# Extraction of V's diagonal blocks in two Vector instructions, and w2 over four column groups in pieces of 4, 5 and 1 rows

## The chip, the cores and the metric

The kernel runs on one NeuronCore of a Trainium2 chip. The metric is the device time of one execution in microseconds (us); lower is better. The engines are named as the profile names them: PE (matrix products; PEld is its weight load), DVE (the Vector engine), ACT (the Scalar engine), POOL (GpSimd) and SP (the queue that issues nearly all DMAs).

## The reference, cut to what matters

The kernel computes one decode step of a gated mix of an attention block and a dense block, for a batch of two rows with 512 features, in bf16:

```
g   = sigmoid(sum(x * gate_w))                      # one gate per batch row
q   = x @ wq                                        # 32 heads of 128
p   = softmax(q . k_cache / sqrt(128))              # 4096 keys per head
a   = (p . v_cache) @ wo                            # wo is 4096 x 512
h   = relu(x @ w1)                                  # 1376 wide
b   = h @ w2                                        # w2 is 1376 x 512
out = g * a + (1 - g) * b                           # 2 x 512
```

The K cache and the V cache hold 64 MB each (2 x 32 heads x 4096 keys x 128 features). All inputs together are about 145 MB, and each byte is used once.

## The kernel before, in words

**Staging.** K and V come in 16 units of 4 MB each (four heads to a unit), K's first, into three slots of `kv`. `wq` comes ahead of them. SP issues every one of these transfers in the order of a list (lines 260 to 271): the transfer of unit n waits until unit n-3 has released its slot, which for a V unit is the marker `pe_v_{v}`, the end of its matrix products. After the last V unit SP issues, without any further wait of its own kind, the last 96 rows of `w2` (`w2a`, line 267), `wo` in two halves (`wo0`, `wo1`, lines 268 and 269), and then the first 1280 rows of `w2` in three pieces (`w2b`, `w2c`, `w2d`, lines 270 and 271). In the tile `w2` a "row" is one slice `w2[:, r, :]` of 128 partitions by 512 columns; `w2b` holds rows 0 to 3, `w2c` rows 4 to 7, `w2d` rows 8 and 9, and row 10 is `w2a`.

**Order.** The program is written out by hand as one list of operations for each engine; an operation waits for named markers of other engines (`waits`) and for the semaphores of transfers (`dwaits`). Each engine works through its list in order.

**K stage.** DVE transposes the 4 MB of a unit in four steps (line 379), PE computes scores from them (lines 385 and 406).

**V stage.** After the softmax, `v_unit(v)` issues 32 matrix products of 512 columns each (line 456) for each V unit. They go to four column groups of the array in turn (group t writes PSUM partitions 32t to 32t+15), so that four run side by side. The result is one PSUM bank of 128 x 512 in which only some 128-column blocks are wanted: for each partition one of four. `v_extract(v)` picks it out with four DVE instructions on 128 columns each: the first multiplies block 0 by column 0 of the mask `maskc` (line 467), each of the next three multiplies block c by column c and adds what is there already (line 470). The result goes to `X2`.

**Where V's transfers are waited for.** For units 1 to 12 the wait for a unit's transfer stands not at its first matrix product on PE but at the last extraction instruction of the unit before, on DVE (line 472); PE waits for that instruction. For units 0 and 13 to 15 the first matrix product itself waits for the transfer (line 459). `o_gather(0)` is issued after unit 8: PE gathers batch row 0's eight results (line 484), DVE scales them (line 488), PE moves them to 128 partitions (line 492), DVE copies them (line 495).

**The end.** After unit 15 come `o_gather(1)`, then `project()`: DVE clears a PSUM bank (line 499), PE multiplies by `wo` in 32 products of 512 columns over four column groups (line 503), rows 16 to 31 of them behind `wo1`, and DVE copies the bank to `pr_sb` (line 506). `ffn_f()` multiplies by `w2`: for each row `fin_row` issues two products of 256 columns, in column groups 0 and 1 (line 510). The order is row 10, rows 0 to 3, then a product of `sel2` with `pr_sb` in float32 that adds the attention's part, then rows 4 to 9. `store()` casts the two halves to bf16, one on DVE (line 524) and one on ACT (line 525), and SP writes 2 KB out (line 272).

Of the kernel before, what the change touches and what calls it, by code (L numbers as in the profile page):

```python
# [4 lines left out]
ALU = mybir.AluOpType  # L5
ACT = mybir.ActivationFunctionType
AX = mybir.AxisListType
# [78 lines left out]
def bass_gated_mix__gqa_block_cached__dense_activation_relu__decode_kernel(  # L86
# [48 lines left out]
    pr_sb = sb("pr_sb", [128, 512], dt.float32)  # L135
# [4 lines left out]
    maskc = sb("maskc", [128, 4], dt.float32)  # L140
# [3 lines left out]
    X2 = sb("X2", [128, 2, 8, 128], dt.float32)  # L144
# [3 lines left out]
    out_sb = sb("out_sb", [2, 512], dt.bfloat16)  # L148
# [6 lines left out]
    def psf(p0, p1, c0, n):  # L155
        return PSF[p0:p1, c0:c0 + n]

    BANK = 512
    V_B = 6
# [9 lines left out]
    FIN_C0 = 0  # L169
# [5 lines left out]
    sem = {n: nc.alloc_semaphore("sem_" + n) for n in names}  # L175
# [4 lines left out]
    def marker(name):  # L180
        m = mk.get(name)
        if m is None:
            m = _Marker()
            mk[name] = m
        return m
# [5 lines left out]
    def slot_of(what):  # L191
        return place[what] % NSLOT

    def slot_wait(what):
        return (sem_slot[slot_of(what)], 16 * (place[what] // NSLOT + 1))

    def freed(what):
        kind, u = what
        return marker(f"kt_{4 * u + 3}") if kind == "k" else marker(f"pe_v_{u}")
# [5 lines left out]
    def dve(fn, waits=(), signal=None, dwaits=()):  # L205
        P.add("dve", fn, waits=[marker(w) for w in waits], signal=marker(signal) if signal else None, dwaits=dwaits)

    def act(fn, waits=(), signal=None, dwaits=()):
        P.add("act", fn, waits=[marker(w) for w in waits], signal=marker(signal) if signal else None, dwaits=dwaits)

    def pe(fn, waits=(), signal=None, dwaits=()):
        P.add("pe", fn, waits=[marker(w) for w in waits], signal=marker(signal) if signal else None, dwaits=dwaits)
# [5 lines left out]
         waits=["c_i16z"], signal="c_i16")  # L218
# [5 lines left out]
                                   in_=mask3[:].rearrange("p (t f) h c -> p t f h c", t=4)[:, :, 0],  # L224
                                   pattern=[[-32, 4], [-4, 4], [-1, 4]],
                                   compare_op=ALU.not_equal, fill=1.0, base=0, channel_multiplier=1),
         waits=["c_m3z"], signal="c_m3")
# [3 lines left out]
         waits=["c_s1"], signal="c_s2")  # L231
    pool(lambda g: g.affine_select(out=sell[:], in_=sell[:], pattern=[[16, 2], [2, 8], [32, 4]],
                                   compare_op=ALU.is_ge, fill=0.0, base=1, channel_multiplier=-1),
         waits=["c_s2"], signal="c_sell")
# [3 lines left out]
         waits=["c_s4z"], signal="c_s4")  # L238
# [16 lines left out]
    def sp(fn, waits=(), dwaits=()):  # L255
        P.add("sp", fn, waits=waits, dwaits=dwaits)
# [4 lines left out]
    for n, what in enumerate(order):  # L261
        waits = [freed(order[n - NSLOT])] if n >= NSLOT else []
        sp(lambda e, what=what: e.dma_start(kv[:, slot_of(what), :], unit_in(what)).then_inc(sem_slot[slot_of(what)], 16),
           waits=waits)
# [2 lines left out]
    sp(lambda e: e.dma_start(w2[0:96, 10, :], B_w2[1280:1376, :]).then_inc(sem["w2a"], 16))  # L267
    sp(lambda e: e.dma_start(wreg[:, 0:8192], wo_in[:, 0:8192]).then_inc(sem["wo0"], 16), waits=[marker("pe_h")])  # L268
    sp(lambda e: e.dma_start(wreg[:, 8192:16384], wo_in[:, 8192:16384]).then_inc(sem["wo1"], 16))
    for name, r0, r1 in (("w2b", 0, 4), ("w2c", 4, 8), ("w2d", 8, 10)):  # L270
        sp(lambda e, name=name, r0=r0, r1=r1: e.dma_start(w2[:, r0:r1, :], w2a_in[:, r0:r1, :]).then_inc(sem[name], 16))
    sp(lambda e: e.dma_start(out.rearrange("b s n -> (b s) n"), out_sb[:, :]).then_inc(sem["out"], 16),
       waits=[marker("dve_out"), marker("act_out")])
# [171 lines left out]
    def v_unit(v):  # L445
        grp, u4 = divmod(v, 4)
        what = ("v", v)
        rows = kv[:, slot_of(what), :].rearrange("p (a c r d) -> p a c r d", a=2, c=4, r=16)
        for n in range(32):
            a, r16 = divmod(n, 16)  # L450
            t = n % 4
            waits = []
            if n == 0:
                waits = [f"pt{grp}_{hq}" for hq in range(4)] if u4 == 0 else []
                waits += [f"dve_x{v - 1}_3"] if v >= 1 else ["dve_v0"]
            pe(lambda e, n=n, t=t, a=a, r16=r16, grp=grp, u4=u4, rows=rows: e.matmul(  # L456
                psf(32 * t, 32 * t + 16, V_B * BANK, 512), lhsT=ptm[:, grp % 2, r16, u4, a, :, :],
                rhs=rows[:, a, :, r16, :], start=(n < 4), stop=(n >= 28), tile_position=(0, 32 * t)),
               waits=waits, dwaits=([slot_wait(what)] if n == 0 and not 1 <= v <= 12 else []), signal=(f"pe_v_{v}" if n == 31 else None))

    def v_extract(v):
        b, u8 = divmod(v, 8)
        for c in range(4):
            src = psf(0, 128, V_B * BANK + 128 * c, 128)
            dst = X2[:, b, u8, :]
            if c == 0:
                dve(lambda e, src=src, dst=dst: e.tensor_scalar(out=dst, in0=src, scalar1=maskc[:, 0:1], scalar2=None, op0=ALU.mult),  # L467
                    waits=[f"pe_v_{v}", "dve_maskc"], signal=f"dve_x{v}_0")
            else:
                dve(lambda e, src=src, dst=dst, c=c: e.scalar_tensor_tensor(out=dst, in0=src, scalar=maskc[:, c:c + 1], in1=dst,  # L470
                                                                            op0=ALU.mult, op1=ALU.add),
                    waits=[f"dve_x{v}_{c - 1}"], dwaits=([slot_wait(("v", v + 1))] if c == 3 and v <= 11 else []), signal=f"dve_x{v}_{c}")


    def o_denominators():
        pe(lambda e: e.matmul(psf(0, 64, L_C0, 1), lhsT=sell[:].rearrange("p b u h -> p (b u h)"), rhs=lrow[:, :], start=True, stop=True),
# [5 lines left out]
    def o_gather(b):  # L482
        for u in range(8):
            pe(lambda e, u=u, b=b: e.matmul(psf(0, 32, O_C0, 128), lhsT=selx[:, 28 - 4 * u:60 - 4 * u], rhs=X2[:, b, u, :],  # L484
                                            start=(u == 0), stop=(u == 7)),
               waits=[f"dve_x{8 * b + u}_3"] + (["dve_rinv", "dve_selx"] if u == 0 else []),
               signal=(f"pe_O{b}" if u == 7 else None))
        dve(lambda v, b=b: v.tensor_scalar(out=O_sb[:, b, :], in0=psf(0, 32, O_C0, 128), scalar1=rinv[:, b:b + 1],  # L488
                                           scalar2=gb[0:32, b:b + 1], op0=ALU.mult, op1=ALU.mult),
            waits=[f"pe_O{b}", "dve_rinv", "dve_g"], signal=f"dve_O{b}")  # L490
        for dq in range(4):
            pe(lambda e, dq=dq, b=b: e.matmul(psf(0, 128, R_C0 + 32 * b, 32), lhsT=s4[:, dq, :], rhs=O_sb[:, b, 32 * dq:32 * dq + 32],  # L492
                                              start=(dq == 0), stop=(dq == 3), tile_position=(0, 0)),
               waits=([f"dve_O{b}", "c_s4"] if dq == 0 else []), signal=(f"pe_R{b}" if dq == 3 else None))
        dve(lambda v, b=b: v.tensor_copy(out=oW[:, :, b], in_=psf(0, 128, R_C0 + 32 * b, 32)), waits=[f"pe_R{b}"], signal=f"dve_oW{b}")
# [10 lines left out]
        dve(lambda v: v.tensor_copy(out=pr_sb[:, :], in_=psf(0, 128, PR_C0, 512)), waits=["pe_pr"], signal="dve_pr")  # L506

    def fin_row(first, last, lhsT, rhs, dw, waits, signal):
        for c in range(2):
            pe(lambda e, c=c: e.matmul(psf(32 * c, 32 * c + 2, FIN_C0, 256), lhsT=lhsT, rhs=rhs[:, c * 256:(c + 1) * 256],  # L510
                                       start=first, stop=last, tile_position=(0, 32 * c), skip_group_check=True),
               dwaits=(dw if c == 0 else []), waits=(waits if c == 0 else []), signal=(signal if c == 1 else None))

    def ffn_f():
        for n, r in enumerate([10, *range(10)]):
            m = 96 if r == 10 else 128
            dw = {10: [(sem["w2a"], 16)], 0: [(sem["w2b"], 16)], 4: [(sem["w2c"], 16)], 8: [(sem["w2d"], 16)]}.get(r, [])
            if r == 4:
                fin_row(False, False, sel2[:, :], pr_sb, [], ["dve_pr", "dve_sel2"], None)
            fin_row(n == 0, r == 9, hT[0:m, r, :], w2[0:m, r, :], dw, ["dve_h0", "dve_h1"] if n == 0 else [],  # L520
                    "pe_fin" if r == 9 else None)

    def store():
        dve(lambda v: v.tensor_copy(out=out_sb[:, 0:256], in_=psf(0, 2, FIN_C0, 256)), waits=["pe_fin"], signal="dve_out")
        act(lambda a: a.activation(out=out_sb[:, 256:512], in_=psf(32, 34, FIN_C0, 256), func=ACT.Copy), waits=["pe_fin"],  # L525
            signal="act_out")


    gate()
# [7 lines left out]
    for v in range(16):  # L537
        if v == 2:
            o_denominators()
        if v % 4 == 0 and 4 <= v <= 8:  # L540
            sm_spread(v // 4 + 1)
        v_unit(v)
        if v == 1:
            ffn_h()
            ffn_relu()
        v_extract(v)
        if v == 8:
            o_gather(0)
    o_gather(1)
    project()  # L550
    ffn_f()
    store()

    P.resolve()
# [30 lines left out]
```

## Time and profile before

| what | value |
|---|---|
| median of 3 runs | 346.12 us (346.08, 346.12, 346.93) |
| the profiled execution: its own time | 346.78 us |
| its span (first to last instruction) | 345.4 us |
| PE, DVE busy share of the span | 58%, 53% |
| DMA: bytes read, mean rate | 145.43 MB, 421 GB/s |
| hardware queue q1, share of 16 DMA engines | 98.3% |
| granted PE clock, mean | 0.822 of full speed |

The profile's durations come from the one profiled execution. The 1.38 us between its time and its span lie outside what the trace shows. In the timeline a row is a run of like instructions: start, stretch in us, engine, line, operation, output and inputs, how many, and in brackets how long the engine idled before it and what ended the idle time.

### The profile page before, as it was taken

The page shows a single profiled execution, that of the slowest core. Times are in us where ns is not written, and L with a number is a line of the kernel's source. Part 1 is how long each engine was busy: PE and PEld are TensorE (multiplying, and loading weights), DVE is VectorE, ACT ScalarE, POOL GpSimd, SP SyncE. Part 2 cuts the span into 40 slices and gives each one's busy share as a digit, 9 for nine tenths or more (in the row PEclk, how much of TensorE's full clock was granted, in tenths as well). Part 3 has the DMA queues.
Part 4 walks back from the last instruction along what each step waited for, and adds up shares of the span by engine and source line. Part 5 has one row for each costly group of instructions (what it writes and reads, how often), then busy time and mean ns, then how long its engine had stood idle before and what let it go on. Part 6 is the DMA issues. An engine that isn't in the chain of part 4 may idle for free.

```text
span 345.4 us, 2397 instructions
## 1 busy us (share of the span) xinstructions
PE 201.0 (58%) x1203; PEld 40.2 (12%) x830; DVE 184.4 (53%) x167; ACT 15.0 (4%) x50; POOL 25.7 (7%) x32
## 2 busy tenths in 40 slices
PE   0429877878788687878780773233445343232365
PEld 0200000000000000000000241000113111000132
DVE  0848998999998999999978121111111201111121
ACT  1040000000000000000004000000000000000000
POOL 8400000000000000000002400400040000000000
PEclk9999998999999999999997565665557866655678
DMA  8999999999999999999999999999999999999994
GB/s 312 452 436 436 429 423 425 433 429 440 440 433 431 422 425 425 436 436 436 433 423 425 433 431 440 433 429 435 429 425 429 435 425 436 436 434 433 392 417 190
DMA packets 5748, 145.58 MB, mean 421 GB/s; under 512 B 645, under 2 KB 746, under 8 KB 1130
## 3 DMA queue, kind: packets, MB, share of 16 engines
q1 hardware_dynamic: 5732, 145.43, 98.3%
q8 instruction: 8, 0.13, 0.2%
q10 hardware_dynamic: 6, 0.00, 0.0%
q14 instruction: 2, 0.02, 0.0%
HBM read 145.43 MB, written 0.00 MB: 421 GB/s over the span
## 4 chain that ended last, share of the span: by engine, by line
DMA 73%; DVE 18%; PE 7%; issue 1%; SPq 1%; ACT 0%; DVEq 0%
DMA kv<-in_A_k_cache_dram 36%; DMA kv<-in_A_v_cache_dram 27%; DVE kt L379 15%; DMA wreg<-in_A_wo_dram 10%; PE PS L456 5%; DVE mpad L414 1%; PE PS L510 1%; DVE kt L427 1%; DVE ptm L440 1%; PE PS L503 1%; DVE X L470 0%; PE PS L385 0%; SPq L267 0%; PE PS L406 0%; SPq L268 0%
## 5 line engine op out<-in xcount | busy, mean ns | idle before, releaser
L379 DVE STREAM_TRANSPOSE kt<-kv 128x2048 f32<-128x2048 f32 x64 | 142.3, 2280 | 18.9 <-DMA kv<-in_A_k_cache_dram 18.9
L385 PE MATMUL PS<-kt,qbuf 128*128 128x512 bf16 x373 | 106.7, 393 | 0.3
L456 PE MATMUL PS<-kv,ptm 128*16 128x512 bf16 x512 | 55.9, 616 | 85.0 <-DVE X L470 57.1
L406 PE MATMUL PS<-kt,qbuf 128*128 128x512 bf16 x128 | 51.1, 399 | 33.5 <-DVE kt L379 32.9
L467 DVE TENSOR_SCALAR X<-PS,maskc 128x128 f32<-128x128 f32 x16 | 5.6, 350 | 67.8 <-PE PS L456 67.8
L470 DVE SCALAR_TENSOR_TENSOR X<-PS,maskc,X 128x128 f32<-128x128 f32 x48 | 16.8, 351 | 46.0 <-DMA kv<-in_A_v_cache_dram 44.7
L442 POOL COPY ptm<-kt 32x512 bf16<-32x512 bf16 x13 | 14.4, 1111 | 232.7 <-DVE lrow L428 175.5
L456 PEld LDWEIGHTS PS<-kv,ptm 128*16 128x16 bf16 x512 | 16.4, 124 | 123.9 <-issue 68.9
L406 PEld LDWEIGHTS PS<-kt,qbuf 128*128 128x128 bf16 x128 | 12.6, 98 | 147.5 <-DVE kt L379 106.6
L349 ACT ACTIVATE qbuf<-PS 32x4 bf16<-32x4 bf16 x32 | 5.7, 179 | 76.6 <-PE PS L385 76.0
L525 ACT ACTIVATE out_sb<-PS 2x256 bf16<-2x256 f32 x1 | 0.4, 375 | 154.6 <-PE PS L510 154.6
L424 ACT ACTIVATE kt<-PS,negm 128x512 bf16<-128x512 f32 x4 | 2.7, 685 | 80.7 <-DVE negm L421 80.7
L279 PE MATMUL PS<-ident,x_sb 3*128 3x3 bf16 x4 | 0.3, 166 | 8.1 <-DMA x_sb<-in_gate_w_dram 8.1
L282 DVE COPY xT<-PS 128x12 bf16<-128x12 bf16 x1 | 0.2, 170 | 8.4 <-PE PS L279 8.4
L503 PE MATMUL PS<-wreg,oW 128*2 128x512 bf16 x32 | 2.9, 500 | 2.9 <-DMA wreg<-in_A_wo_dram 2.0
L220 POOL MEMSET qbuf<- 128x5120 bf16 x1 | 4.4, 4370 | 0.0
L484 PE MATMUL PS<-X,selx 128*32 128x128 f32 x32 | 4.0, 273 | 0.1
L284 DVE COPY xTw<-xT 128x8 bf16<-128x8 bf16 x1 | 4.0, 3973 | 0.0
L365 DVE TENSOR_SCALAR hT<-PS,gm 128x10 bf16<-128x10 f32 x2 | 0.5, 226 | 6.3 <-PE PS L359 6.3
L492 PE MATMUL PS<-O_sb,s 32*128 32x32 bf16 x8 | 0.5, 182 | 5.5 <-DVE O_sb L488 5.5
L318 PE MATMUL PS<-wreg,xTw 128*32 128x512 bf16 x32 | 3.6, 628 | 0.0
L285 DVE TENSOR_TENSOR xg<-xT 128x8 f32<-128x8 bf16 x1 | 3.6, 3630 | 0.0
(66 smaller groups left out, 49.5 us busy)
## 6 DMA issues: line engine op xcount, KB each, us to landing
kv<-in_A_k_cache_dram SPq DMA_DIRECT2D x16, 4096.0 KB, 20.6
kv<-in_A_v_cache_dram SPq DMA_DIRECT2D x16, 4096.0 KB, 25.0
wreg<-in_A_wq_dram SPq DMA_DIRECT2D x1, 4096.0 KB, 12.4
wreg<-in_A_wo_dram SPq DMA_DIRECT2D x2, 2048.0 KB, 31.7
wreg<-in_B_w_dram SPq DMA_DIRECT2D x1, 1376.0 KB, 23.1
w<-in_B_w_dram SPq DMA_DIRECT2D x2, 512.0 KB, 35.1
w<-in_B_w_dram SPq DMA_DIRECT2D x1, 256.0 KB, 35.6
w<-in_B_w_dram SPq DMA_DIRECT2D x1, 96.0 KB, 25.4
```

Of the source, the lines that this page charges most:

```text
L220: pool(lambda g: g.memset(qbuf[:], 0.0), signal="c_qbuf")
L284: dve(lambda v: v.tensor_copy(out=xTw[:, :, 0:2], in_=xT), waits=["dve_xT", "c_xTw"], signal="dve_xTw")
L349: act(lambda a, out=out, src=src: a.activation(out=out, in_=src, func=ACT.Copy), waits=[f"pe_sc_{4 * uh + 3}"], signal=f"q_1_{uh}_{hq}")
L379: dve(lambda v: v.transpose(out=dst, in_=pairs[:, h, 64 * rr:64 * rr + 64, :]), waits=([f"pe_sc_{i - NKT}"] if i >= NKT else []), dwaits=( ...
L385: return e.add_instruction(mybir.InstMatmult(start_tensor_calc=start, stop_tensor_calc=stop, tile_size=(128, 128), tile_position=(0, 0), l ...
L406: return e.matmul(out, lhsT=lhsT, rhs=rhs, start=start, stop=stop)
L442: pool(lambda e, dst=dst, src=src: e.tensor_copy(out=dst, in_=src), waits=waits, signal=f"pt{g}_{hq}")
L456: pe(lambda e, n=n, t=t, a=a, r16=r16, grp=grp, u4=u4, rows=rows: e.matmul(psf(32 * t, 32 * t + 16, V_B * BANK, 512), lhsT=ptm[:, grp % 2, ...
L467: dve(lambda e, src=src, dst=dst: e.tensor_scalar(out=dst, in0=src, scalar1=maskc[:, 0:1], scalar2=None, op0=ALU.mult), waits=[f"pe_v_{v}" ...
L470: dve(lambda e, src=src, dst=dst, c=c: e.scalar_tensor_tensor(out=dst, in0=src, scalar=maskc[:, c:c + 1], in1=dst, op0=ALU.mult, op1=ALU.add),
L484: pe(lambda e, u=u, b=b: e.matmul(psf(0, 32, O_C0, 128), lhsT=selx[:, 28 - 4 * u:60 - 4 * u], rhs=X2[:, b, u, :], start=(u == 0), stop=(u ...
L503: pe(lambda e, r=r, t=t: e.matmul(psf(32 * t, 32 * t + 2, PR_C0, 512), lhsT=oW[:, r, :], rhs=wreg[:, r * 512:(r + 1) * 512], start=(r < 4) ...
```

## The change

Three parts.

1. `v_extract` becomes two DVE instructions. A `tensor_tensor` multiplies the whole 128 x 512 bank by `maskc`, each of its four columns broadcast over 128 features, into `pr_sb` (free until the end); a `tensor_reduce` adds the four blocks, read with the block index innermost (a stride of 128 elements), into `X2`. DVE no longer waits for the next unit's transfer: the first product of every V unit waits for it on PE.
2. `w2` comes in pieces of 4, 5 and 1 rows instead of 4, 4 and 2, and `fin_row` issues four products of 128 columns in column groups 0 to 3 instead of two of 256 columns.
3. `store` casts four quarters instead of two halves: quarters 0 and 1 on DVE, 2 and 3 on ACT.

```diff
-    for name, r0, r1 in (("w2b", 0, 4), ("w2c", 4, 8), ("w2d", 8, 10)):
+    for name, r0, r1 in (("w2b", 0, 4), ("w2c", 4, 9), ("w2d", 9, 10)):
...
-                waits += [f"dve_x{v - 1}_3"] if v >= 1 else ["dve_v0"]
+                waits += [f"dve_x{v - 1}"] if v >= 1 else ["dve_v0"]
...
-               waits=waits, dwaits=([slot_wait(what)] if n == 0 and not 1 <= v <= 12 else []), signal=(f"pe_v_{v}" if n == 31 else None))
+               waits=waits, dwaits=([slot_wait(what)] if n == 0 else []), signal=(f"pe_v_{v}" if n == 31 else None))
...
-        for c in range(4):
...
-                dve(lambda e, src=src, dst=dst: e.tensor_scalar(out=dst, in0=src, scalar1=maskc[:, 0:1], scalar2=None, op0=ALU.mult),
...
-                dve(lambda e, src=src, dst=dst, c=c: e.scalar_tensor_tensor(out=dst, in0=src, scalar=maskc[:, c:c + 1], in1=dst,
...
-                    waits=[f"dve_x{v}_{c - 1}"], dwaits=([slot_wait(("v", v + 1))] if c == 3 and v <= 11 else []), signal=f"dve_x{v}_{c}")
+        parts = pr_sb[:, :].rearrange("p (c d) -> p c d", c=4)
+        dve(lambda e: e.tensor_tensor(out=parts, in0=psf(0, 128, V_B * BANK, 512).rearrange("p (c d) -> p c d", c=4),
+                                      in1=maskc[:].unsqueeze(2).to_broadcast([128, 4, 128]), op=ALU.mult),
+            waits=[f"pe_v_{v}", "dve_maskc"], signal=f"dve_m{v}")
+        dve(lambda e: e.tensor_reduce(out=X2[:, b, u8, :], in_=parts.rearrange("p c d -> p d c"), axis=AX.X, op=ALU.add),
+            waits=[f"dve_m{v}"], signal=f"dve_x{v}")
...
-        for c in range(2):
-            pe(lambda e, c=c: e.matmul(psf(32 * c, 32 * c + 2, FIN_C0, 256), lhsT=lhsT, rhs=rhs[:, c * 256:(c + 1) * 256],
+        for c in range(4):
+            pe(lambda e, c=c: e.matmul(psf(32 * c, 32 * c + 2, FIN_C0, 128), lhsT=lhsT, rhs=rhs[:, c * 128:(c + 1) * 128],
...
-            dw = {10: [(sem["w2a"], 16)], 0: [(sem["w2b"], 16)], 4: [(sem["w2c"], 16)], 8: [(sem["w2d"], 16)]}.get(r, [])
+            dw = {10: [(sem["w2a"], 16)], 0: [(sem["w2b"], 16)], 4: [(sem["w2c"], 16)], 9: [(sem["w2d"], 16)]}.get(r, [])
...
-        dve(lambda v: v.tensor_copy(out=out_sb[:, 0:256], in_=psf(0, 2, FIN_C0, 256)), waits=["pe_fin"], signal="dve_out")
-        act(lambda a: a.activation(out=out_sb[:, 256:512], in_=psf(32, 34, FIN_C0, 256), func=ACT.Copy), waits=["pe_fin"],
-            signal="act_out")
+        for c in range(2):
+            dst, src = piece(c)
+            dve(lambda v, dst=dst, src=src: v.tensor_copy(out=dst, in_=src), waits=["pe_fin"], signal=("dve_out" if c else None))
+        for c in range(2, 4):
+            dst, src = piece(c)
+            act(lambda a, dst=dst, src=src: a.activation(out=dst, in_=src, func=ACT.Copy), waits=["pe_fin"],
+                signal=("act_out" if c == 3 else None))
```

`piece(c)` is the pair of `out_sb[:, 128 * c:128 * c + 128]` and PSUM partitions 32c and 32c+1, columns 0 to 127.

More of the change, by code (lines that the diff above doesn't have):

```diff
@@ L458, in v_unit @@
                 rhs=rows[:, a, :, r16, :], start=(n < 4), stop=(n >= 28), tile_position=(0, 32 * t)),
-               waits=waits, dwaits=([slot_wait(what)] if n == 0 and not 1 <= v <= 12 else []), signal=(f"pe_v_{v}" if n == 31 else None))
+               waits=waits, dwaits=([slot_wait(what)] if n == 0 else []), signal=(f"pe_v_{v}" if n == 31 else None))
     def v_extract(v):
         b, u8 = divmod(v, 8)
-        for c in range(4):
-            src = psf(0, 128, V_B * BANK + 128 * c, 128)
-            dst = X2[:, b, u8, :]
-            if c == 0:
-                dve(lambda e, src=src, dst=dst: e.tensor_scalar(out=dst, in0=src, scalar1=maskc[:, 0:1], scalar2=None, op0=ALU.mult),
-                    waits=[f"pe_v_{v}", "dve_maskc"], signal=f"dve_x{v}_0")
-            else:
-                dve(lambda e, src=src, dst=dst, c=c: e.scalar_tensor_tensor(out=dst, in0=src, scalar=maskc[:, c:c + 1], in1=dst,
-                                                                            op0=ALU.mult, op1=ALU.add),
-                    waits=[f"dve_x{v}_{c - 1}"], dwaits=([slot_wait(("v", v + 1))] if c == 3 and v <= 11 else []), signal=f"dve_x{v}_{c}")
+        parts = pr_sb[:, :].rearrange("p (c d) -> p c d", c=4)
[4 more added lines that the diff above has]
+            waits=[f"dve_m{v}"], signal=f"dve_x{v}")
     def o_denominators():
@@ L485, in o_gather @@
                                             start=(u == 0), stop=(u == 7)),
-               waits=[f"dve_x{8 * b + u}_3"] + (["dve_rinv", "dve_selx"] if u == 0 else []),
+               waits=[f"dve_x{8 * b + u}"] + (["dve_rinv", "dve_selx"] if u == 0 else []),
                signal=(f"pe_O{b}" if u == 7 else None))
@@ L508, in fin_row @@
     def fin_row(first, last, lhsT, rhs, dw, waits, signal):
-        for c in range(2):
-            pe(lambda e, c=c: e.matmul(psf(32 * c, 32 * c + 2, FIN_C0, 256), lhsT=lhsT, rhs=rhs[:, c * 256:(c + 1) * 256],
+        for c in range(4):
+            pe(lambda e, c=c: e.matmul(psf(32 * c, 32 * c + 2, FIN_C0, 128), lhsT=lhsT, rhs=rhs[:, c * 128:(c + 1) * 128],
                                        start=first, stop=last, tile_position=(0, 32 * c), skip_group_check=True),
-               dwaits=(dw if c == 0 else []), waits=(waits if c == 0 else []), signal=(signal if c == 1 else None))
+               dwaits=(dw if c == 0 else []), waits=(waits if c == 0 else []), signal=(signal if c == 3 else None))
     def ffn_f():
@@ L523, in store, with piece @@
     def store():
-        dve(lambda v: v.tensor_copy(out=out_sb[:, 0:256], in_=psf(0, 2, FIN_C0, 256)), waits=["pe_fin"], signal="dve_out")
-        act(lambda a: a.activation(out=out_sb[:, 256:512], in_=psf(32, 34, FIN_C0, 256), func=ACT.Copy), waits=["pe_fin"],
-            signal="act_out")
+        def piece(c):
+            return out_sb[:, 128 * c:128 * c + 128], psf(32 * c, 32 * c + 2, FIN_C0, 128)
+        for c in range(2):
[5 more added lines that the diff above has]
+                signal=("act_out" if c == 3 else None))
     gate()
```

## The prediction, made blind

> **What bounds the kernel now.** I read the page's slices first, then the chain of waits, then the timeline of the last 6 us.
>
> ```profile
> DMA  8999999999999999999999999999999999999994
> HBM read 145.43 MB, written 0.00 MB: 421 GB/s over the span
> ...
> 190.00:330.00 140.00, 58.00 (x554) 20.28 (x558) 22.45 (x69) 0.00 (x0) 12.48 (x12) 0.61 1.00 429
> 339.20:342.60 3.40, 3.06 (x28) 1.21 (x30) 0.69 (x1) 0.00 (x0) 0.00 (x0) 0.50 0.53 207
> 342.60:345.40 2.80, 1.09 (x16) 0.51 (x12) 0.41 (x1) 0.38 (x1) 0.00 (x0) 1.00 0.00 1
> ```
>
> The first two lines are of the page, the others of the table by stretches (length, busy time of PE, PEld, DVE, ACT, POOL, granted clock, DMA share, GB/s). From slice 2 to the last the 16 DMA engines are full. In the V stage (190 to 330) PE is busy 58 of 140 us and DVE 22, at a DMA share of 1.00. So V's instructions can grow or shrink by microseconds without moving the end. The queues q1 and q8 are busy 98.3% + 0.2% of 345.4 us, 340.2 us per engine, and the stream runs from some 1.8 us to the last landing at 342.65 (below): all the holes in it come to about 0.6 us.
>
> The end is the part that nothing covers:
>
> ```profile
> 339.49 0.04 issue
> 339.54 1.88 PE PS L503 x16
> 341.42 2.29 PE PS L510 x23
> 343.71 0.02 issue
> 343.73 0.41 DVE out_sb L524
> ```
>
> ```profile
> 336.47 1.03 PE L503 MATMUL PS<-wreg,oW 128*2 128x512 bf16 x16 [0.88 <-DVE PS L499]
> 339.54 1.88 PE L503 MATMUL PS<-wreg,oW 128*2 128x512 bf16 x16 [2.03 <-DMA wreg<-in_A_wo_dram]
> 341.20 1.27 PE L510 MATMUL PS<-w,hT 96*2 96x256 bf16 x10
> 341.47 0.69 DVE L506 COPY pr_sb<-PS 128x512 f32<-128x512 f32 x1 [5.05 <-PE PS L503]
> 342.27 0.76 PE L510 MATMUL PS<-pr_sb,sel 128*2 128x256 f32 x4
> 342.87 0.82 PE L510 MATMUL PS<-w,hT 128*2 128x256 bf16 x12
> 343.73 0.38 ACT L525 ACTIVATE out_sb<-PS 2x256 bf16<-2x256 f32 x1 [154.59 <-PE PS L510]
> ```
>
> The first block is the chain (start, length, who), the second the timeline. The chain's last wait is for the second half of `wo`, which lands at 339.49. Then come 16 products, ten of `w2`, the copy of the bank, the float32 product, twelve of `w2`, the casts and the output. In 339.2 to 342.6 the granted clock was 0.50, and the same 16 products took 1.88 us instead of 1.03. The three pieces of `w2` are issued at 306.06, 306.53 and 307.01 and take 34.7, 35.5 and 35.6 us (line 271's landings): they land at 340.77, 342.0 and 342.65. In this execution none of them was waited for: `w2d`'s first product started 342.87 + 4 x 0.109 = 343.30.
>
> **Part 1, the extraction.** Four instructions go (350 ns each; from 332.87 to 334.38, 1.51 us with their waits on one another). Two come. The product reads 512 columns of PSUM: line 506 copies as many in 0.69 us; four times line 470's 0.35 is 1.40, the upper end. I take 0.70, the row of equal size. The sum reads 512 float32 with a stride. Unstrided, line 300 (128 in 0.28 us) extended by line 414's 2292/2048 = 1.1 ns an element gives 0.68. With a stride the small reductions give more: line 287 reads 8 in 0.160, line 302 32 in 0.208, 2.0 ns an element, hence 0.208 + 480 x 0.002 = 1.17. I take 1.1, since they are strided. Together 1.4 to 2.6 us, likely 1.8: 0.3 longer than now. The Trainium skill ("VectorE: DVE Perf Modes", section "Rules for kernel authors") advises fewer DVE instructions, which the change follows, and to restructure a `tensor_reduce` on a hot path, which it violates; no row here shows this reduce. By that page's one element per cycle of 0.96 GHz (an estimate) 512 elements are 0.53 us and the start; either way the next paragraph hides it.
>
> What hides it: in the V stage a unit lands every 9.8 us and takes 3.6 us of PE, so DVE has some 6. After the last unit the extraction is followed by gather, copies, clearing and the first 16 `wo` products, which end 337.5; `wo1` lands 339.49. The cover is 1.99 us, against at most 1.1 more. Without it each 0.1 us would be 0.1 us at the end.
>
> The moved wait: PE now waits for a V unit's transfer itself. At 212.40 the landing released DVE, 0.36 us of extraction ran, PE began at 212.87; now PE begins some 0.4 us earlier, as unit 13's did (0.11 after its landing), and after unit 8 by 1.0 us, since lines 488 and 492 no longer stand between. Behind the waiting product on PE are only the unit's own products and what follows them; nobody waits for those sooner. DVE, which had `o_gather(0)`'s instructions behind its wait, is freed. SP issues the next unit 0.4 us earlier, but two others are in its queue (a V transfer takes 25.0 us from issue to landing, 2.5 units of 9.8). With the DMA share at 1.00 the worth lies between 0 and the 0.6 us of holes; I take 0.
>
> **Part 2, the w2 rows and pieces.** Bytes are the same, so `w2d`, now 128 KB, still lands last, near 342.65; `w2c` carries 128 KB more, 0.30 us at 430 GB/s, and lands near 342.3.
>
> The time of a row: four column groups are on record with 512 columns (16 products in 1.03 us at full clock, four rounds, hence (1.03 - 0.378)/3 = 0.215 from round to round, line 503's shortest product being 0.377 long). Two groups of 256: last twelve products 0.82 - 0.273 = 0.547 over five steps, 0.109 a row. Both are 0.42 ns a column of one group: groups run side by side. Four groups of 128 aren't on record: 0.055 if only columns count; 0.109 if starting a product costs as much as now; 0.22 if they ran one after another. I take 0.055, by line 503's row. Line 492's four products of 32 columns started (0.26 - 0.17)/3 = 0.03 us apart, within one group, so a floor of 0.03 each (0.12 a row) can't be excluded. The Trainium skill ("TensorE: Matmul & The Clock Gate", section "Wait — 56ns, not 53.3ns?") puts a floor of about 25 ns between starts, which speaks against a gain: 0.10 a row by it. But line 503's sixteen need 64 ns each anyway, so no row here decides whether the floor holds across groups.
>
> *At half clock, as profiled.* Row 10 and rows 0 to 3 take 5 x 0.107 instead of 5 x 0.213 and are done at 341.74, but the float32 product waits for the copy (341.47 + 0.69): it starts 342.22 instead of 342.27, gain 0.05. It needed 0.60 us, 0.33 at half clock and 0.27 at full, 0.435 in full-clock time; half the columns per group need 0.218, and begun at 342.22 that is 0.38 at half clock and 0.03 more: gain 0.20. Rows 4 to 9: five steps of 0.055 instead of 0.109, gain 0.27, and the last product is 0.05 shorter. Sum 0.57. Row 4 would start 342.62, after `w2c`; row 9 at 342.9, after `w2d`. With 0.109 a row the sum is 0.30.
>
> *At full clock.* Sixteen products from 339.54 end 340.57; copy until 341.3; float32 product until 341.8; row 4 then waits for `w2c` (342.0), row 8 for `w2d` until 342.70. Two rows more: 342.70 + 0.109 + 0.273 = 343.08, which is 0.61 before the profiled 343.69. That gives 346.78 - 0.61 = 346.17: the median, 346.12. So I read the runs at 346.08 and 346.12 as ones whose last microseconds had the full clock, and those at 346.9 and 346.78 as ones with half. Here the landing is the bound, and the change gains one row and the shorter product: 0.109 + 0.054 = 0.16.
>
> **Part 3, the casts.** 256 columns took 0.41 on DVE and 0.38 on ACT. With line 349's 0.178 for 4 columns, ACT's slope is 0.197/252, so 128 columns take 0.275. Line 349's four follow each other at 0.79 us in all, 0.20 apart: 0.025 between them. Two on ACT: 0.275 + 0.3 = 0.575. DVE: 128 columns 0.28, two at most 0.60, at least 0.47 (lines 365 and 368 start before their predecessor's end). The store becomes 0.16 us longer, between 0.06 and 0.25; nothing hides it.
>
> **The sum.** Full clock: 346.12 - 0.16 + 0.16 = 346.1. Half clock: 346.78 - 0.57 + 0.16 = 346.4. The profiled execution is 0.66 above the median because of the clock, so by these runs the full-clock case is the commoner: I predict 346.1.
>
> **Rivals.** (a) The half-clock case is the commoner one after the change: 346.4. For it: PE still stands idle ahead of `wo1`. Against: two of three runs.
> (b) Slower: four groups of 128 run one after another, 0.22 a row at full clock. At full clock rows 0 to 3 end 341.7, the float32 product takes 0.85 (342.55), rows 4 to 9 1.32: the last ends 344.0 instead of 343.08, with the casts +1.1: 347.2. At half clock the same sum is +1.8: 348.6. It decides from about 0.2 us a row. Against it: line 503's four groups run side by side.
> (c) Faster: earlier releases close the stream's holes. Price at most 0.6, with the half-clock gain of 0.41 some 1.0: 345.1. Against it: share 1.00 all through the V stage.
> (d) The pieces don't do what they say: `w2d` as a small last piece lands no earlier, and with 0.109 a row only the casts remain: 346.3.
>
> **Chances.** Forecast 0.50, (a) 0.18, (d) 0.14; these lie within 0.3% (1.04 us), about what a measurement of this kernel can tell from no change. (b) 0.11, (c) 0.07, of which 0.05 lies beyond 0.3% (more holes than I count) and 0.02 within. Faster 0.05, same 0.84, slower 0.11. The range leaves out (b) and most of (c), 0.16 in all: 345.4 to 347.1, which holds the half-clock case and all ends of the row's and the casts' prices.
>
> **What would show it.** Right: last landing near 342.65, `w2`'s last product within 0.3 us of it plus 0.22 at full clock, casts ending 0.55 to 0.6 after it, a V unit's first product some 0.1 us after its landing, extraction near 1.8 us. Wrong: `w2` rows 0.2 us apart, a DMA slice under 9 ahead of the last, `wo1` landing away from 339.5 by over 0.5, or the first 16 `wo` products ending after `wo1` lands.

## The result, and the profile after

The kernel after the change has a median of 345.78 us (345.51 to 345.97, 11 runs), the kernel before 346.36 us (345.98 to 346.93, 11 runs). The ratio is 0.998, with a 95% interval of 0.9971 to 0.9989: about 0.6 us or 0.2% faster, inside the 0.3% band. The times before spread over 1.0 us, those after over 0.5 us.

The first fence is from the page of the kernel after (granted PE clock and DMA share in 40 slices, then the read rate), the second is its DMA queue section (queue, packets, MB, share). Before, the read rate was 421 GB/s and the row of q14 had "2, 0.02".

```profile
PEclk9999998999999999999997565665556866555678
DMA  8999999999999999999999999999999999999995
HBM read 145.43 MB, written 0.00 MB: 422 GB/s over the span
```

```profile
q1 hardware_dynamic: 5732, 145.43, 98.5%
q8 instruction: 8, 0.13, 0.2%
q14 instruction: 1, 0.01, 0.0%
```

The DMA engines are as full as before, and the bytes are the same. One thing is missing: queue q14, which reads instructions, fetched one page of 8 KB (at 115.4 us) instead of two (116.7 and 304.4 us before). The experiments ask whether this matters.

In the V stage (190 to 330) the table by stretches has PE busy 59 us and DVE 27, at a DMA share of 1.00, as before:

```profile
190.00:330.00 140.00, 58.90 (x558) 21.00 (x562) 26.98 (x38) 0.00 (x0) 12.20 (x12) 0.60 1.00 429
```

The end of the kernel after, by its chain and then by its timeline:

```profile
339.00 0.04 issue
339.05 1.90 PE PS L498 x15
340.95 0.02 issue
340.97 0.70 DVE pr_sb L501
341.68 0.04 issue
341.72 0.96 PE PS L505 x32
```


```profile
332.45 0.69 DVE L464 TENSOR_TENSOR pr_sb<-PS,maskc 128x512 f32<-128x512 f32 x1 [8.43 <-PE PS L456]
333.18 1.03 DVE L467 TENSOR_REDUCE X<-pr_sb 128x128 f32<-128x512 f32 x1
...
336.30 1.03 PE L498 MATMUL PS<-wreg,oW 128*2 128x512 bf16 x16 [0.88 <-DVE PS L494]
339.05 1.88 PE L498 MATMUL PS<-wreg,oW 128*2 128x512 bf16 x16 [1.71 <-DMA wreg<-in_A_wo_dram]
...
340.71 0.75 PE L505 MATMUL PS<-w,hT 96*2 96x128 bf16 x20
...
340.97 0.69 DVE L501 COPY pr_sb<-PS 128x512 f32<-128x512 f32 x1 [4.73 <-PE PS L498]
...
341.72 0.60 PE L505 MATMUL PS<-pr_sb,sel 128*2 128x128 f32 x8 [0.26 <-DVE pr_sb L501]
...
342.10 0.56 PE L505 MATMUL PS<-w,hT 128*2 128x128 bf16 x24
342.70 0.55 ACT L527 ACTIVATE out_sb<-PS 2x128 bf16<-2x128 f32 x2 [153.88 <-PE PS L505]
342.70 0.57 DVE L524 CAST out_sb<-PS 2x128 bf16<-2x128 f32 x2 [1.04 <-PE PS L505]
```

In the chain the copy of the bank (line 501) now stands between the `wo` products and the float32 product, where before PE's own `w2` rows stood: rows 10 and 0 to 3 take half the time and PE waits for the copy, as forecast. The extraction takes 1.76 us (332.45 to 334.21) and is hidden: the first 16 `wo` products still end at 337.3, the second half of `wo` lands at 339.00. From there to the end of the span pass 344.5 - 339.0 = 5.5 us, against 345.4 - 339.5 = 5.9 before: from the landing to the last product the `w2` rows gained 0.54 (4.20 us became 3.66), and the casts gave 0.16 back. The rest of the 0.9 us between the two spans lies ahead of that: the stream itself was 0.5 us earlier (the second half of `wo` 339.00 instead of 339.49, `w2`'s last piece 342.18 instead of 342.65). The two profiled executions alone can't say whether that is the change or chance; the landing marks below say more.

### The profile page after: what moved, and what is told of

The parts are those of the page before. It is cut to its first block, busy times and chain, and to the rows that moved or that the text cites. A ratio compares the mean times of both kernels' runs of the same rounds, so it can differ in the third digit from the quotient of the medians.

```text
span 344.5 us, 2426 instructions
## 1 busy us (share of the span) xinstructions
PE 201.8 (59%) x1240; PEld 40.6 (12%) x856; DVE 189.6 (55%) x136; ACT 15.2 (4%) x51; POOL 25.7 (7%) x32
## 4 chain that ended last, share of the span: by engine, by line
DMA 72%; DVE 18%; PE 7%; issue 1%; SPq 1%; ACT 0%; DVEq 0%
DMA kv<-in_A_k_cache_dram 35%; DMA kv<-in_A_v_cache_dram 27%; DVE kt L379 16%; DMA wreg<-in_A_wo_dram 10%; PE PS L456 5%; PE PS L385 1%; DVE mpad L414 1%; DVE kt L427 1%; DVE ptm L440 1%; PE PS L498 1%; PE PS L406 0%; SPq L263 0%; PE PS L505 0%; DVE pr_sb L501 0%; DVE out_sb L524 0%
## 5 line engine op out<-in xcount | busy, mean ns | idle before, releaser
L385 PE MATMUL PS<-kt,qbuf 128*128 128x512 bf16 x384 | 109.4, 393 | 0.0
L464 DVE TENSOR_TENSOR pr_sb<-PS,maskc 128x512 f32<-128x512 f32 x16 | 11.1, 691 | 108.6 <-PE PS L456 108.6
L406 PE MATMUL PS<-kt,qbuf 128*128 128x512 bf16 x128 | 51.1, 399 | 32.3 <-DVE kt L379 32.3
L467 DVE TENSOR_REDUCE X<-pr_sb 128x128 f32<-128x512 f32 x16 | 16.3, 1021 | 0.5
L479 PEld LDWEIGHTS PS<-X,selx 128*32 128x32 f32 x32 | 3.4, 110 | 1.3 <-DVE X L467 0.6
```

The costliest lines, as they stand in the source:

```text
L385: return e.add_instruction(mybir.InstMatmult(start_tensor_calc=start, stop_tensor_calc=stop, tile_size=(128, 128), tile_position=(0, 0), l ...
L406: return e.matmul(out, lhsT=lhsT, rhs=rhs, start=start, stop=stop)
L464: dve(lambda e: e.tensor_tensor(out=parts, in0=psf(0, 128, V_B * BANK, 512).rearrange("p (c d) -> p c d", c=4), in1=maskc[:].unsqueeze(2). ...
L467: dve(lambda e: e.tensor_reduce(out=X2[:, b, u8, :], in_=parts.rearrange("p c d -> p d c"), axis=AX.X, op=ALU.add), waits=[f"dve_m{v}"], s ...
```

## The experiments

Two theories of the stream were tried first. TAIL: the gain comes from `w2`'s rows alone, and the earlier stream is chance. STREAM: the extraction part makes the stream earlier, by the earlier release of the slots, or by the shorter DVE program. The kernel before ran again beside each group of runs, and each median is given with the one it had there. That median was 346.14 to 346.38 from group to group, so a run is compared within its group.

### Each part alone, and the moved wait alone

e1 has part 1 of the change alone:

```diff
-               waits=waits, dwaits=([slot_wait(what)] if n == 0 and not 1 <= v <= 12 else []), signal=(f"pe_v_{v}" if n == 31 else None))
+               waits=waits, dwaits=([slot_wait(what)] if n == 0 else []), signal=(f"pe_v_{v}" if n == 31 else None))
...
+        dve(lambda e: e.tensor_reduce(out=X2[:, b, u8, :], in_=parts.rearrange("p c d -> p d c"), axis=AX.X, op=ALU.add),
```

> Only part 1 of the change (two-instruction extraction, V's waits on PE); w2 and the casts as before. Theory TAIL (the 0.6 us come from w2's rows, part 2; the stream's end moving from 342.65 to 342.18 in the two profiled executions is scatter): no change, 0.0 +- 0.15 us against before. Theory STREAM (part 1 lets the DMA stream end some 0.4 us earlier): -0.3 to -0.5 us, with the second half of wo landing near 339.0 instead of 339.5.

Measured: 346.01 us (345.66 to 346.62), before 346.25; ratio 0.9988 (0.9979 to 0.9998).

e2 has parts 2 and 3 alone (`v_unit` and `v_extract` as before):

```diff
-    for name, r0, r1 in (("w2b", 0, 4), ("w2c", 4, 8), ("w2d", 8, 10)):
+    for name, r0, r1 in (("w2b", 0, 4), ("w2c", 4, 9), ("w2d", 9, 10)):
...
-        for c in range(2):
+        for c in range(4):
```

> Only parts 2 and 3 (w2 over four column groups in pieces of 4, 5 and 1 rows, four casts); extraction and V's waits as before. TAIL: -0.4 to -0.6 us against before, from landing of wo's second half to the end 5.5 us instead of 5.9. STREAM: -0.1 to -0.3 us, and the second half of wo lands near 339.5.

Measured: 346.02 us (345.80 to 346.44), before 346.25; ratio 0.9991 (0.9982 to 0.9999).

e3 is the kernel before with the wait moved and nothing else:

```diff
-               waits=waits, dwaits=([slot_wait(what)] if n == 0 and not 1 <= v <= 12 else []), signal=(f"pe_v_{v}" if n == 31 else None))
+               waits=waits, dwaits=([slot_wait(what)] if n == 0 else []), signal=(f"pe_v_{v}" if n == 31 else None))
...
-                    waits=[f"dve_x{v}_{c - 1}"], dwaits=([slot_wait(("v", v + 1))] if c == 3 and v <= 11 else []), signal=f"dve_x{v}_{c}")
+                    waits=[f"dve_x{v}_{c - 1}"], signal=f"dve_x{v}_{c}")
```

> The kernel before with one thing changed: the wait for a V unit's transfer is taken from DVE's last extraction instruction and put on the unit's first product on PE; four extraction instructions stay. TAIL: 0.0 +- 0.15 us. STREAM by the earlier release of the slots: -0.3 to -0.5 us. STREAM by the smaller number of DVE instructions: 0.0.

Measured: 346.01 us (345.63 to 346.80), before 346.25; ratio 0.9990 (0.9980 to 1.0000).

e8 has the two-instruction extraction with the wait left on DVE:

```diff
-            waits=[f"dve_m{v}"], signal=f"dve_x{v}")
+            waits=[f"dve_m{v}"], dwaits=([slot_wait(("v", v + 1))] if v <= 11 else []), signal=f"dve_x{v}")
```

> The kernel before with the two-instruction extraction, but the wait for the next V unit's transfer left on DVE (on the sum); w2 and casts as before. TAIL: 0.0 +- 0.15 us. STREAM by the earlier release: 0.0, or +0.1 since the sum of 1.02 us now stands between a landing and PE. STREAM by fewer DVE instructions (before, 8 KB of code were fetched at 304.4, after not): -0.3 to -0.5 us.

Measured: 346.16 us (345.67 to 346.68), before 346.25; ratio 0.9991 (0.9981 to 1.0001).

What follows: each half of the change is worth about 0.23 us by its median, with intervals that nearly reach zero, and neither theory has it all. e2 fell short of what TAIL gives, e1 of what STREAM gives. e8 fell furthest short: it lost the second page, and its 0.09 us can't be told from nothing. Two things show in the traces. First, the second half of `wo` landed at 339.5 in the kernel before and in e2 (two pages of q14), and at 339.2 to 339.3 in e1, e3 and e8. These three fetched no second q14 page during the run (e3, too, has a shorter DVE program, the waits on transfers being gone from it: its second page came at 346.6, after the last instruction). The pages don't settle the landing by themselves, though: e5 below fetched two, the second at 304.2, and landed at 339.30. Second, the times of e1, e3 and e8 spread into an upper and a lower group (clearest in e3: eight of 345.63 to 346.16, four of 346.65 to 346.80), and the clock of the last microseconds goes with the group. The table by stretches for 339.3 to 342.4, first e1 (its execution took 346.01), then e3 (346.76):

```profile
339.30:342.40 3.10, 2.82 (x38) 0.99 (x38) 0.69 (x1) 0.00 (x0) 0.00 (x0) 1.00 0.50 194
```

```profile
339.30:342.40 3.10, 3.10 (x30) 1.27 (x32) 0.69 (x1) 0.00 (x0) 0.00 (x0) 0.56 0.52 199
```

The seventh number is the granted clock, 1.00 and 0.56. `w2`'s last piece landed at 342.48 and 342.36, so the streams differ by 0.1 us the other way; the last product ended at 342.90 and 343.58. The other profiled executions with `w2` in two column groups agree: half clock in the kernel before (346.78), full clock in e8 (345.88) and e5 (346.09).

### The clock at the end

e5 and e6 keep PE busy where it waits for the second half of `wo` (e5 on the kernel before, e6 on the kernel after):

```diff
+            if r == 15:
+                for f in range(16):
+                    pe(lambda e, f=f: e.matmul(psf(32 * (f % 4), 32 * (f % 4) + 2, 3 * BANK, 512), lhsT=oW[:, 0, :], rhs=wreg[:, 0:512],
+                                               start=True, stop=True, tile_position=(0, 32 * (f % 4))))
```

> The kernel before plus 16 filler products (the operands of the first wo product, into an unused PSUM bank) behind the first 16 wo products, where PE waits some 2 us for the second half of wo. Theory CLOCK (the upper half of the times before, near 346.8, are executions whose last 3.4 us had half clock because PE stood idle there; at full clock w2's last landing decides): clock 1.00 from wo's second half on, all runs in the lower group, 345.9 to 346.3, median 346.05, last product 0.43 us after w2's last landing. Theory SCATTER (the spread comes from the DMA stream): median as before, 346.25, runs up to 347.2.

> The kernel after the change plus the same 16 filler products. CLOCK: 0.0 to -0.15 us against the kernel after (345.78), all runs within 0.4 us; last product 0.27 us after w2's last landing. SCATTER: as after, 345.78.

Measured: e5 346.21 us (345.94 to 346.44, 11 runs) beside 346.14 (345.76 to 347.24, 33 runs) for the kernel before, ratio 1.0001 (0.9993 to 1.0010); e6 345.84 us (345.49 to 346.00), ratio 0.9989 (0.9981 to 0.9998). e5 by its timeline:

```profile
337.45 1.04 PE L508 MATMUL PS<-wreg,oW 128*2 128x512 bf16 x16
339.34 1.03 PE L503 MATMUL PS<-wreg,oW 128*2 128x512 bf16 x16 [0.85 <-DMA wreg<-in_A_wo_dram]
...
341.87 1.02 PE L514 MATMUL PS<-w,hT 128*2 128x256 bf16 x12
342.51 0.09 PEld L514 LDWEIGHTS PS<-w,hT 128*2 128x2 bf16 x4 [0.34 <-DMA w<-in_B_w_dram]
342.94 0.37 ACT L529 ACTIVATE out_sb<-PS 2x256 bf16<-2x256 f32 x1 [154.14 <-PE PS L514]
```

With the filler the 16 products behind the wait take 1.03 us instead of 1.88, rows 8 and 9 wait for the last piece, and the last product ends 0.42 us after it lands (342.47 to 342.89). CLOCK holds for the upper group. Of e5's runs one in 11 is above 346.4, where the kernel before has 9 in the 33 beside it and 33 in all 91; that alone could be chance. But with e10 and e12 below, which also have two column groups and the filler (with other pieces of `w2`), it is one in 33 (346.44), against 10 in the 35 of e1, e3 and e8 without it, and all profiled executions with the filler had the clock at 1.00. The median of e5 isn't 346.05, and it isn't below that of before: this part of the expectation missed by 0.16 us, and why is open. On the kernel after, the filler changes nothing in the time that can be measured (345.84 with it, 345.78 and 345.81 without it in other groups of runs), though the two profiled executions without it had the clock at half. In e6 the four rows of `w2b` run at full clock:

```profile
340.62 0.39 PE L509 MATMUL PS<-w,hT 128*2 128x128 bf16 x16 [0.19 <-DMA w<-in_B_w_dram]
```

### The pages of DVE's code

e9 gives the kernel after a DVE program about as long as before; e11 the same with 22 in place of 6 (and a `pad` of 352 columns):

```diff
+        for f in range(6):
+            dve(lambda e, f=f: e.memset(pad[:, 6 * v + f:6 * v + f + 1], 0.0))
```

> The kernel after the change plus six tiny DVE instructions (a memset of 128x1 to a column that nobody reads) behind each unit's extraction, some 0.6 us of DVE in each unit, hidden: DVE's program is about as long as before again. Theory CODE (a second 8 KB page of DVE's code, read at 304.4 in the kernel before, holds up one DMA engine and thereby every later landing by 0.3 us): the page is read again, wo's second half lands near 339.5, time +0.3 us against after: 346.1. Rival WAIT (the stream is earlier since the slots are released earlier): page read again, landing stays near 339.0 to 339.2, time as after, 345.8.

> The kernel after the change plus 22 tiny DVE instructions behind each unit's extraction (352 in all, some 0.4 us of DVE a unit, hidden): DVE's program grows by 22 KB, so about three more 8 KB pages of its code are read during the V stage than in the kernel after. Theory CODE, all pages on one DMA engine: +0.33 us a page, +0.9 us against after (346.7). CODE, pages spread over the engines: the last landing moves by one page at most, +0.2 to +0.4 (346.1). WAIT (the stream's end depends on when slots are released, not on code): 0.0 against after (345.8).

> The kernel after the change once more, as the yardstick of the other runs of this job: 345.8, within 0.15 us, all runs within 0.5 us of one another; against before -0.5 us where half of before's executions have half clock at the end.

Measured: e9 346.16 us (345.72 to 346.43; ratio to before 0.9997, 0.9988 to 1.0006) beside 345.84 for e6; e11 347.88 us (347.63 to 348.70, 6 runs; ratio to before 1.0048, 1.0035 to 1.0062) beside 345.81 (345.60 to 346.16) for the kernel after run again, e14 (the kernel before had 346.38 there, so e14's ratio is 0.9985, 0.9977 to 0.9994; its spread of 0.56 us is 0.06 more than expected). The queue rows of e9 and of e11:

```profile
q14 instruction: 2, 0.02, 0.0%
```

```profile
q14 instruction: 4, 0.03, 0.0%
```

The page that e9 adds is read at 259.5 us, those of e11 at 212.1, 260.4 and 318.4: they come and move with DVE's program, so q14 carries DVE's code there. Time goes with the pages: one more page 0.32, three more 2.07. The interval of e9 still touches that of e6; e11 settles it. PE's wait for the second half of `wo` ends later with each, in e6, e9 and e11:

```profile
339.34 1.03 PE L498 MATMUL PS<-wreg,oW 128*2 128x512 bf16 x16 [0.30 <-DMA wreg<-in_A_wo_dram]
```

```profile
339.63 1.03 PE L501 MATMUL PS<-wreg,oW 128*2 128x512 bf16 x16 [1.49 <-DMA wreg<-in_A_wo_dram]
```

```profile
341.43 1.03 PE L501 MATMUL PS<-wreg,oW 128*2 128x512 bf16 x16 [0.81 <-DMA wreg<-in_A_wo_dram]
```

The price isn't bandwidth, since three pages are 24 KB of 145 MB. It is one DMA engine. The table by stretches of e11, last stretches (DMA share and GB/s are the last two numbers):

```profile
337.00:339.20 2.20, 1.21 (x11) 0.77 (x9) 0.85 (x11) 0.00 (x0) 0.00 (x0) 0.92 0.99 407
339.20:342.30 3.10, 1.91 (x36) 0.67 (x36) 0.33 (x1) 0.00 (x0) 0.00 (x0) 1.00 0.53 206
342.30:344.50 2.20, 1.27 (x52) 0.57 (x44) 0.69 (x1) 0.00 (x0) 0.00 (x0) 1.00 0.05 20
```

From 342.3 to 344.5 a share of 0.05 is about one engine in sixteen (1/16 = 0.06). A transfer of 128 partitions lands in sixteen parts, each with its own mark in the trace: of those of the second half of `wo` fifteen lie between 337.04 and 339.09, and one at 341.38. A mark doesn't name its engine, but the marks of one transfer can be laid beside those of the transfer before it. In e11 the page at 212.1 takes one mark from 1.34 us behind the first to 2.31, the page at 260.4 takes the latest from 2.31 to 3.33, the page at 318.4 from 3.31 to 4.29: 1.0 us each, on one and the same mark. Every later transfer lands with it, and PE waits.

What the end pays is that 1.0 us less the lead that the engine had over the latest one. In e11 the lead was 0.63, and three pages less 0.63 are 2.3 (the landing came 2.1 later than in e14). In e9 the page at 259.5 takes a mark from 1.43 to 2.44, past a latest of 2.19, so the end pays about 0.2. In e2 the page at 304.4 goes 0.41 past the latest, in e5 the one at 304.2 goes 0.14 past it. In the profiled execution of the kernel before it takes a mark from 1.25 to 2.22, and the latest stands at 2.27 before and after: there the second page cost the end nothing, and its landing at 339.49 has another cause. So a second page costs 0 to 0.4 us at the end from one execution to the next; 0.32 (e9) and 0.24 (e1) are what the medians give. WAIT (the release of the slots) is refuted: e9 has V's waits on PE, as the kernel after has, and lands at 339.59; e8 has the old release and lands at 339.19.

The same marks explain the spread at the end of the stream, eight marks some 1.5 us behind the other eight. In the kernel after one mark is more than 0.8 us behind the first after the page of queue q8 at 48.6 us (16 KB), three after the pages at 110.8 (q8) and 115.4 (q14), and then one more after each further page of q8 (173.5, 203.8, 245.0, 270.3, 322.7): eight pages, eight late marks. A page of q8 takes a mark back by about 1.5 us, each time another one.

### Other divisions of w2

e10 has part 1, the pieces of 4, 5 and 1 rows and the filler, but `w2` in two column groups of 256 columns and two casts:

> Part 1 of the change and the pieces of 4, 5 and 1 rows, but w2's rows in two groups of 256 columns and two casts as before, with the 16 filler products. CLOCK: at full clock the landing decides; after it 0.05 + 0.27 + 0.41 us (one row, halves cast) instead of 0.05 + 0.22 + 0.57 with four groups: 0.1 us faster than the kernel after with fillers, 345.6. If four groups are worth something at full clock: slower than that kernel by 0.1 to 0.3.

Measured: 345.99 us (345.86 to 346.20; ratio to before 0.9994, 0.9985 to 1.0003), beside 345.84 for e6: the other sign, 0.15 us slower. Its timeline, from the landing of `w2c`:

```profile
342.19 0.82 PE L509 MATMUL PS<-w,hT 128*2 128x256 bf16 x12 [0.37 <-DMA w<-in_B_w_dram]
343.05 0.38 ACT L524 ACTIVATE out_sb<-PS 2x256 bf16<-2x256 f32 x1 [154.02 <-PE PS L509]
```

The last piece landed at 342.49, but six rows at 0.109 from 342.19 on kept PE busy until then and past it; the last product ended 0.52 us after the landing. With five rows in the piece ahead of the last one, two groups are too slow. e12 therefore has two groups with other pieces (the line taken out is that of the kernel after):

```diff
-    for name, r0, r1 in (("w2b", 0, 4), ("w2c", 4, 9), ("w2d", 9, 10)):
+    for name, r0, r1 in (("w2b", 0, 4), ("w2c", 4, 6), ("w2e", 6, 9), ("w2d", 9, 10)):
```

> Part 1 of the change, w2's rows in two groups of 256 columns, two casts, 16 filler products, and w2 in pieces of 4, 2, 3 and 1 rows. In the run with pieces of 4, 5 and 1 and two groups the five rows (5 x 0.109 = 0.55 us) were still running when the last piece landed 0.34 us after the one before. If that is why four groups won there: last product 0.32 us after w2's last landing, casts 0.41 after it, 0.1 us faster than the kernel after, 345.7. Rival (two groups lose for another reason): last product over 0.45 us after the last landing, 346.0.

Measured: 345.81 us (345.63 to 345.98; ratio to before 0.9986, 0.9977 to 0.9995), as the kernel after beside it (345.81). The last product ended 0.31 us after the last landing, as expected, and the casts took 0.41; the 0.1 us that this should bring doesn't show in the median. No version here is faster than the change.

e13 sends rows 0 to 3 of `w2` in 16 transfers of 8 partitions:

```diff
+    for p8 in range(16):
+        sp(lambda e, p8=p8: e.dma_start(w2[8 * p8:8 * p8 + 8, 0:4, :], w2a_in[8 * p8:8 * p8 + 8, 0:4, :]).then_inc(sem["w2b" if p8 < 8 else "w2e"], 16))
```

> The kernel after with w2's rows 0 to 3 (512 KB) sent as 16 transfers of 8 partitions each, in the place of one of 128. In every trace so far eight DMA engines end some 1.6 us before the other eight (the 16 increments of wo's second half: eight at 337.1 to 337.6, eight at 338.2 to 339.5). If a transfer of 8 partitions goes to eight engines only and these are the early ones: w2's last landing 0.4 us earlier, 345.4. If they are the late ones or mixed: last landing 1 us later or more, 346.5 or more. If such a transfer is spread over all 16: as after, 345.8.

Measured: 349.02 us (348.70 to 349.15, 4 runs), before 346.38; ratio 1.0077 (1.0063 to 1.0091). The second half of `wo` landed at 340.2 and `w2`'s last piece at 345.3, 2.9 us after that of the unchanged kernel beside it (342.4): the case "late ones or mixed", and more. Such transfers do not fill the early engines; which engines they use stays open. Why eight engines run ahead is told above: by the count of marks they are those that carried no page of instructions.

## Why the prediction was right, and where it was not

The time, 345.78, lies in the range, and the change within 0.3%, as forecast; the point, 346.1, was 0.3 too high. One of the signs of being wrong, `wo1` landing over 0.5 from 339.5, was missed narrowly (339.00).

- **The bound.** Right. V's extraction became 0.25 us longer and stayed hidden: 1.76 us against 1.8 forecast, with 0.69 for the product (0.70) and 1.03 for the strided sum (1.1; the unstrided 0.68 was too low).
- **The moved wait, worth "between 0 and the 0.6 us of holes; I take 0".** For the mechanism that was priced, the release of the slots, nothing in the runs speaks against 0 (e8 and e9 above). Nor were the 0.6 us holes to be closed: in the kernel before the sixteen marks of `w2d` lie on average 1.2 us ahead of the latest (342.65), so engines that ended early account for all of it. (Units land 9.7 us apart, not 9.8.) But the same edit takes waits and instructions out of DVE's program, and with them a page of code. This is the term that failed: I had counted no price for a program's length. By the medians it is worth 0.2 to 0.3 us (e9 against e6 0.32, e1 0.24; e8, 0.09, can't be told from nothing), most of the distance between 346.1 and 345.78. The trace of before lists the page, at 304.4 on q14; I summed q8 with q1 and looked no further. In that very execution it happened to cost nothing, so its end would not have shown the price; the steps in the landing marks would. The 0.49 us between the two profiled landings of `wo1` (339.49 and 339.00) is therefore no measure of this term.
- **Row time.** Right, and rival (b) is out. At half clock twenty products, the last of them 0.31 long, take 0.75 us: (0.75 - 0.31)/4 = 0.11 a row (0.107 forecast). The last 24, ending with one of 0.22, take (0.56 - 0.22)/5 = 0.07 a row, the first of them held up by the float32 product. At full clock, in e6, the sixteen products of four rows take 0.39, the last of them 0.22: (0.39 - 0.22)/3 = 0.057 a row (0.055 forecast), 14 ns a product. So four groups run side by side at 128 columns, and the floor per started product that I weighed doesn't hold across groups.
- **Half clock and full clock.** Right. The profiled executions with full clock at the end (e1, e5) end their last product 0.42 us after the last landing, the four-group ones (e2, e6) 0.26: gain 0.16, as worked out. At half clock 5.9 us became 5.5 (0.36; 0.41 forecast). The full-clock case was the commoner for the kernel before, if its upper group is the half-clock one: 58 of its 91 runs are at most 346.4. Since the rest had half clock, the shorter rows also lower the median: e2 shows 0.23 with one run in 11 above 346.4 (346.44), where a forecast for the commoner case alone gives 0. The median before, 346.12 of three runs, was itself the full-clock value; over eleven runs it is 346.36, which the prediction could not know. After the change both profiled executions without filler (the kernel after and e14) had half clock: as far as two executions tell, rival (a) was right on the clock and wrong on its price.
- **The casts.** 0.57 us instead of 0.41, as forecast (0.16), though DVE ends last, not ACT.
- **Rival (c)**, earlier releases closing holes, did not happen (e8 lands as early without them, e9 late with them); **(d)** is refuted by the row time.

## What to carry to other kernels

Where the DMA stream has no holes, look at what else uses the DMA engines: here each page of instructions set one of them back, and the transfers that came after landed with that engine. A shorter program can be worth more than shorter instructions. And behind the last wait, size pieces and rows together: the rows of one piece must be done before the next lands, or the small last piece brings nothing.

## What the runs showed of the hardware

- An 8 KB page of DVE's code set one landing mark back by 0.97 to 1.02 us (seven pages in the kernel before, e2, e5, e9 and e11), though its own transfer is recorded with 0.33 us. The end pays what exceeds the engine's lead over the latest one: 0 to 0.4 us for a second page, 2.07 us for three more (e11). The Trainium skill ("Runtime: NRT & Kernel Launch", section "Instruction fetch mechanics") says that crossing a block of 16 KB costs one DMA tail-bump and is mostly hidden. Here a page is 8 KB on q14, and its fetch is not hidden from the data: the measurement decides.
- The sixteen DMA engines don't end together: in the kernel after the second half of `wo` has eight landing marks from 337.2 to 337.6 and eight from 338.2 to 339.0. In that run the number of late marks grew by one with each page of instructions read (eight pages by then).
- The kernel before had 1.03 us of PE work (16 products) in the 3.4 us ahead of `wo`'s landing and then clock 0.50 from 339.2 to 342.6; e2 had the same work in the 3.4 us ahead of it and clock 1.00 from 339.3 to 342.4. With 16 filler products more the clock stayed at 1.00 in e5, e6, e10 and e12. More work there went with the full clock each time; by what rule the clock is granted, these runs don't show.
